# The modulation's last 2,176 bytes a row loaded in parts of 126, 2, 124 and 4 rows instead of 128

## Chip, cores, metric

One core of one Trainium2 chip. The metric is device time in microseconds (us), lower is better. A run counts as slow when it is over 1.5% above the fastest of the same kernel; such runs are left out of every comparison here.

## The reference

A decode block with adaptive layer norm: modulation, cached grouped attention over 8,192 keys, a gated MLP with ReLU gate. Cut to what matters:

```python
B, Sq, D = 8, 1, 1024; Hq, Hkv, Sk, Dh = 32, 4, 8192, 128; F = 3584
mod = (silu(c) @ w_mod).reshape(B, 6, 1, D)          # w_mod: 1024 x 6144, bf16
sa, ca, ga, sb, cb, gb = (mod[:, i] for i in range(6))
h = layernorm(x) * (1 + ca) + sa
x = x + ga * attention(h, k_cache, v_cache, wq, wo)
h = layernorm(x) * (1 + cb) + sb
x = x + gb * ((relu(h @ W_gate) * (h @ W_up)) @ W_down)
```

Everything is read once: 185.6 MB of weights and caches for a few KB of results.

## The kernel before

One ring of on-chip memory, the arena, takes all large operands in turn. Each is loaded with one instruction over all 128 partitions from the sync engine's queue, as soon as the part of the arena that it overwrites has been read. The chip has 16 DMA engines, and each of these loads is spread over all 16.

```python
wm_src = w_mod.rearrange("(p k) n -> p (k n)", k=KC)       # 128 rows of 98,304 bytes
load(("wm", 0), wm_src[:, 0:D], D, 0)                      #  2,048 bytes a row
load(("wm0", 0), wm_src[:, D:24 * D], 23 * D, D)           # 47,104
load(("wm", 1), wm_src[:, 24 * D:48 * D], 24 * D, 24 * D)  # 49,152
# ... then wq in two halves, for each batch K in two halves and V, then wo, gate, up
wd_parts = [(0, 14), (14, 21), (21, 25), (25, 27), (27, 28)]
for i, (r0, r1) in enumerate(wd_parts):                    # W_down last, in shrinking parts
    load(("wd", i), d_src[:, r0 * D:r1 * D], (r1 - r0) * D, VPART + r0 * D)
```

W_down's last 7 of 28 rows per partition are summed in a bank of their own, so that after the last load (2,048 bytes a row) only 8 small matmuls, two VectorE operations and the store are left.

## Time and profile before

| | before |
|---|---|
| time, first three runs | 436.42 us median (436.19 to 436.79) |
| profiled span | 434.9 us |
| share of the 16 DMA engines' time that the main queue fills | 99.0% |
| last load landed | 432.13 us |

The profile's page gives busy shares in 40 slices and the DMA queues; the view of windows gives busy time by stretch; the chain of waits lists what ended last. Beyond these views the trace keeps every DMA packet (start, duration, size, queue) and every landing, which is the time when one engine has finished its share of one load. A stretch without a packet in between is called a hole. Consecutive packets of one engine follow each other with a constant overlap of 4 ns, so the packets can be sorted into 16 sequences, one per engine. A sequence has no engine number in the trace.

### The profile page before, as it was taken

The page shows a single profiled execution, that of the slowest core. Times are in us where ns is not written, and L with a number is a line of the kernel's source. Part 1 is how long each engine was busy: PE and PEld are TensorE (multiplying, and loading weights), DVE is VectorE, ACT ScalarE, POOL GpSimd, SP SyncE. Part 2 cuts the span into 40 slices and gives each one's busy share as a digit, 9 for nine tenths or more (in the row PEclk, how much of TensorE's full clock was granted, in tenths as well). Part 3 has the DMA queues.
Part 4 walks back from the last instruction along what each step waited for, and adds up shares of the span by engine and source line. Part 5 has one row for each costly group of instructions (what it writes and reads, how often), then busy time and mean ns, then how long its engine had stood idle before and what let it go on. Part 6 is the DMA issues. An engine that isn't in the chain of part 4 may idle for free. (4 is left out here: it accounts for less than half of the span.)

```text
span 434.9 us, 4853 instructions
## 1 busy us (share of the span) xinstructions
PE 260.7 (60%) x2175; PEld 137.3 (32%) x2015; DVE 249.8 (57%) x345; ACT 29.8 (7%) x55; POOL 9.2 (2%) x24
## 2 busy tenths in 40 slices
PE   0325339566838874783977478487838856364247
PEld 0100003163218224421822352172226316241015
DVE  0603059747972985597299649739963974430021
ACT  1100010100020002002000200200020020100000
POOL 3000000000000000000000000000000000000000
PEclk9966569969978996998699599979968986885678
DMA  9999999989999999999999999999999999999996
GB/s 374 452 431 434 433 434 437 471 375 440 440 413 428 455 440 407 434 455 413 431 464 422 416 434 464 410 425 443 458 398 431 443 464 410 448 429 429 427 418 255
DMA packets 5526, 185.74 MB, mean 427 GB/s; under 512 B 720, under 2 KB 784, under 8 KB 1168
## 3 DMA queue, kind: packets, MB, share of 16 engines
q1 hardware_dynamic: 5376, 185.61, 99.0%
q8 instruction: 5, 0.08, 0.1%
q10 hardware_dynamic: 144, 0.04, 0.0%
q14 instruction: 1, 0.01, 0.0%
HBM read 185.63 MB, written 0.02 MB: 427 GB/s over the span
## 5 line engine op out<-in xcount | busy, mean ns | idle before, releaser
L584 DVE STREAM_TRANSPOSE kt<-arena 128x1024 uint32<-128x1024 uint32 x128 | 148.2, 1211 | 62.1 <-DVEq L181 44.7
L594 PE MATMUL ps<-kt,qpad 128*128 128x512 bf16 x512 | 133.9, 384 | 42.8 <-DVE kt L584 36.7
L634 PE MATMUL ps<-arena,pT 128*64 128x256 bf16 x1024 | 74.8, 321 | 51.0 <-PEq L181 51.0
L634 PEld LDWEIGHTS ps<-arena,pT 128*64 128x64 bf16 x1024 | 72.0, 132 | 53.2 <-issue 52.3
L594 PEld LDWEIGHTS ps<-kt,qpad 128*128 128x128 bf16 x512 | 40.5, 98 | 132.3 <-DVE kt L584 99.7
L624 DVE TENSOR_SCALAR pT<-pd,mqf 128x1024 bf16<-128x1024 bf16 x64 | 28.2, 503 | 0.6
L616 ACT ACTIVATE prb<-ps,bias 128x1024 bf16<-128x1024 f32 x16 | 17.7, 1110 | 138.8 <-DVE mjt L611 138.8
L622 DVE STREAM_TRANSPOSE pd<-prb 128x1024 bf16<-128x1024 bf16 x16 | 19.8, 1238 | 10.9 <-ACT prb L616 10.9
L600 DVE TENSOR_REDUCE negm<-ps 128x1 f32<-128x512 f32 x32 | 21.2, 661 | 4.5 <-PE ps L594 4.5
L762 PE MATMUL ps<-arena,hT 128*32 128x448 bf16 x128 | 10.7, 518 | 16.9 <-DMA arena<-in_B_W_up_dram 10.6
L769 DVE TENSOR_TENSOR kt<-ps,kt 128x448 bf16<-128x448 f32 x2 | 1.2, 620 | 27.8 <-PE ps L762 27.8
L546 PE MATMUL ps<-arena,hT 128*32 128x512 bf16 x64 | 7.2, 630 | 12.2 <-DMA arena<-in_A_wq_dram 12.2
L522 PE MATMUL ps<-arena,hT 128*32 128x512 bf16 x96 | 9.0, 551 | 8.2 <-DMA arena<-in_w_mod_dram 8.2
L653 ACT ACTIVATE oacc<-ps 128x32 f32 (+1 forms) x9 | 1.8, 198 | 158.6 <-PE ps L648 158.6
L575 POOL TENSOR_TENSOR qpad<-qR,mq 128x128 bf16<-128x128 bf16 x8 | 4.9, 607 | 310.7 <-DVE pT L624 258.2
L529 DVE COPY mod<-ps 128x512 f32<-128x512 f32 x2 | 1.3, 671 | 16.5 <-PE ps L522 16.5
L762 PEld LDWEIGHTS ps<-arena,hT 128*32 128x32 bf16 x64 | 2.3, 134 | 25.1 <-DMA arena<-in_B_W_up_dram 11.7
L557 DVE CAST kt<-ps 128x512 bf16<-128x512 f32 x1 | 0.7, 692 | 15.9 <-PE ps L546 15.9
L783 PE MATMUL ps<-arena,hmT 128*32 128x256 bf16 x84 | 6.4, 329 | 3.9 <-DMA arena<-in_B_W_down_dram 3.9
L606 PE MATMUL ps<-identf,negm 128*128 128x128 f32 x16 | 3.9, 326 | 7.8 <-DVE negm L604 7.8
L722 PE MATMUL ps<-arena,kt 128*32 128x256 bf16 x128 | 4.9, 328 | 4.6 <-DMA arena<-in_A_wo_dram 4.6
L546 PEld LDWEIGHTS ps<-arena,hT 128*32 128x32 bf16 x32 | 1.2, 137 | 18.2 <-DMA arena<-in_A_wq_dram 14.8
(99 smaller groups left out, 88.9 us busy)
## 6 DMA issues: line engine op xcount, KB each, us to landing
arena<-in_A_k_cache_dram SPq DMA_DIRECT2D x16, 4096.0 KB, 27.2
arena<-in_A_wq_dram SPq DMA_DIRECT2D x2, 4096.0 KB, 34.2
arena<-in_B_W_gate_dram SPq DMA_DIRECT2D x1, 7168.0 KB, 24.2
arena<-in_B_W_up_dram SPq DMA_DIRECT2D x1, 7168.0 KB, 28.8
arena<-in_w_mod_dram SPq DMA_DIRECT2D x1, 6144.0 KB, 30.4
arena<-in_w_mod_dram SPq DMA_DIRECT2D x1, 5888.0 KB, 16.5
arena<-in_B_W_down_dram SPq DMA_DIRECT2D x1, 3584.0 KB, 19.0
arena<-in_B_W_down_dram SPq DMA_DIRECT2D x1, 1792.0 KB, 22.9
```

Of the source, the lines that this page charges most:

```text
L522: fns.append(lambda e, w=w, pr=pr, j=j, kk=kk: hold(e.matmul(ps[32 * j:32 * j + 32, pr, :], hT[:, kk, :], w[:, 2 * pr:2 * pr + 2, j, :], s ...
L546: fns.append(lambda e, w=w, r=kk - r0, z=z, g=g, kk=kk: hold(e.matmul(ps[32 * g:32 * g + 32, 4 + z, :], hT[:, kk, :], w[:, r, g, z, :], st ...
L575: P.op("pool", lambda e: e.tensor_tensor(out=qpad[:, :, 24:152].rearrange("p u (q c) -> p u q c", q=4)[:, :, :, 0:J], in0=qR[:].rearrange( ...
L584: P.op("dve", lambda e_: e_.transpose(ktb[:, to:to + PART].bitcast(dt.uint32), arena[:, lo:lo + PART].bitcast(dt.uint32)), reads=[slot_r(l ...
L594: fns.append(lambda e_, t=t, r=r: e_.matmul(ps[:, e // 4, :].rearrange("p (c k) -> p c k", k=32), qpad[:, t * 2 + r, 24 - 8 * i:152 - 8 * ...
L600: P.op("dve", lambda e: e.tensor_reduce(negm[:, h:h + 1], ps[:, h, :], AX.X, ALU.max, negate=True), reads=[bank(h)] + (free(("ka", b)) if ...
L616: P.op("act", lambda e: e.activation(prb[:, f, :], ps[:, 2 * f:2 * f + 2, :].rearrange("p h n -> p (h n)"), ACT.Exp, bias=bias[:, 0:1], sc ...
L622: P.op("dve", lambda e: e.transpose(pd[:, f], prb[:, f]), reads=[R("prb", f, f + 1)], writes=[R("pd", 1024 * f, 1024 * f + 1024)])
L624: P.op("dve", lambda e, g=g: e.tensor_scalar(out=pT[:, f, :, :, g, :], in0=pd[:, f].rearrange("p (c i x) -> p c i x", c=32, i=2), scalar1= ...
L634: fns.append(lambda e, n=n, h=h, c_=c_, i=i, t=t: e.matmul(ps[64 * t:64 * t + 64, 5, 0:2 * Dh].rearrange("p (i d) -> p i d", d=Dh), pT[:, ...
L762: fns.append(lambda e, w=w, kk=kk, h=h, j=j, b0=b0: hold(e.matmul(ps[32 * j:32 * j + 32, b0 + h, 0:H], hT[:, kk, :], w[:, kk, j, h, :], st ...
L783: fns.append(lambda e, w=w, r=k - r0, k=k, i2=i2, j=j: e.matmul(ps[32 * j:32 * j + 32, 4, 0:256], hmT[:, k, 1 - i2:33 - i2], w[:, r, i2, j ...
```

## The change

The apparent intent: DMA engines 14 and 15 are to have less to move. Each load over 128 rows has one landing from each of the 16 engines and 8 packets on each; the last 2,176 bytes of each row are now loaded with row counts that do not divide evenly over 16 engines.

```diff
+    UNEVEN = [(832, 126), (256, 124)]          # bf16 elements a row, rows of the first part
 ...
-        load(("wm", 1), wm_src[:, 24 * D:48 * D], 24 * D, 24 * D)
+        at1 = 48 * D - sum(n for n, rows in UNEVEN)
+        load(("wm", 1), wm_src[:, 24 * D:at1], at1 - 24 * D, 24 * D)
+        for n, rows in UNEVEN:
+            for lo, part in ((0, slice(0, rows)), (n // 2, slice(rows, 128))):
+                load(("wm1", n, lo), wm_src[part, at1:at1 + n], n // 2, at1 + lo, arena[part, at1:at1 + n])
+            at1 += n
```

The rest of the diff hands a destination through the load helper. The two parts of a strip claim half of the strip's columns each in the kernel's own bookkeeping; the matmuls read all of them, so they wait for all four.

More of the change, by code (lines that the diff above doesn't have):

```diff
@@ L382, in bass_adaLN_cond__gqa_block_cached__glu_gated_reglu__decode_kernel, with load @@
         stream, place = [], {}
-        def load(key, src, n, lo):
+        def load(key, src, n, lo, dst=None):
             place[key] = lo
-            stream.append((key, src, n, lo))
+            stream.append((key, src, n, lo, arena[:, lo:lo + n] if dst is None else dst))
         def pump():
             while stream:
-                key, src, n, lo = stream[0]
+                key, src, n, lo, dst = stream[0]
                 if P.unread("arena", lo, lo + n):
@@ L393, in pump @@
                 stream.pop(0)
-                dst = arena[:, lo:lo + n]
                 P.op("sp", lambda e, dst=dst, src=src: e.dma_start(dst, src), writes=[slot_r(lo, lo + n)], dma=True,
```

## The prediction

> **What bounds the kernel now.** I read the page's header and its slices first. The DMA row shows nines from the second slice to the last but one and the compute engines stay far below that, so the 16 DMA engines are the candidate for the bound.
>
> ```profile
> span 434.9 us, 4853 instructions
> PE 260.7 (60%) x2175; PEld 137.3 (32%) x2015; DVE 249.8 (57%) x345; ACT 29.8 (7%) x55; POOL 9.2 (2%) x24
> DMA  9999999989999999999999999999999999999996
> ...
> q1 hardware_dynamic: 5376, 185.61, 99.0%
> q8 instruction: 5, 0.08, 0.1%
> q14 instruction: 1, 0.01, 0.0%
> ```
>
> To be seen here: one queue carries 185.61 MB in packets that fill 99.0% of all 16 engines' time, and beside it there are six small packets called instruction (five of 16,384 bytes, one of 8,192). The busy times by stretch agree: between 95 and 340 us the DMA share is 1.00 at 434 GB/s, PE is busy 170 us of 245 and VectorE 173.
>
> ```profile
> 95.00:340.00 245.00, 169.78 (x1293) 95.14 (x1288) 173.39 (x224) 15.19 (x31) 3.77 (x6) 0.89 1.00 434
> ```
>
> Then the DMA issue queue's own waits and its timeline, to see whether that queue ever runs dry. The gate weights are issued at 374.19 us and the transfer ahead of them (wo) lands at 381.27, so 7 us of work still stood in the rings; that lead is among the smallest. In the prologue the first half of K is issued at 36.40 us and wq's second half lands at 52.16; K's second half is issued at 55.84, when the first of the engines needs still 4.3 us for the half before it (its first share lands at 60.11). So compute never starves the DMA engines, and a shift of under 1 us in compute is absorbed.
>
> Last the chain that ended last and its timeline at the end.
>
> ```profile
> 405.43 24.84 DMA arena<-in_B_W_down_dram
> 430.26 0.04 issue
> 430.31 1.07 PE ps L792 x32
> 431.38 0.34 PE ps L746 x4
> 431.72 0.87 PE ps L792 x24
> 432.59 0.02 issue
> 432.61 0.29 DVE lu L803
> ```
>
> The pieces after the DMA are one short tail: W_down's last three loads land at 430.26, 431.49 and 432.13 us by the records of landings, PE ends at 432.6, two VectorE operations and the store finish at 434.83. The tail starts when the LAST of 16 engines has delivered its share. So the time is: the slowest DMA engine's stream plus a fixed tail of 2.7 us. What matters is therefore which engine is slowest, and that I read from the trace itself: every load has 16 landings (one per engine), and the packets of one engine follow each other so exactly (4 ns overlap) that the 16 sequences of 296 packets can be told apart.
>
> In the final load, 11 engines land by 430.94 or so and five much later: 431.97, 432.00, 432.10, 432.10, 432.13. All five delays have the same origin. At 46.40, 96.15, 386.53, 397.29 and 428.70 us one sequence, each time another, has a packet prolonged by 482 to 550 ns and then a hole of 861 to 935 ns, 1.42 us together; each is at one of the five 16,384-byte instruction packets (45.47, 95.28, 385.67, 396.35, 427.78). The 8,192-byte one (76.92) costs a sixth engine 0.83 us. The lost time is never made up, because the rings are never empty. The trace has no engine numbers, so I cannot see which numbers the five have.
>
> **What the Trainium skill says.** "Runtime: NRT & Kernel Launch", section Instruction fetch mechanics: instruction memories are refilled in 16 KiB blocks through a DMA queue driven by the sequencer. The trace agrees: five packets of exactly 16,384 bytes, on queues of their own. "DMA: Bandwidth & Descriptors", Queues, rings and completion order: each engine takes turns between its queues and the queues share the 16 engines. The trace agrees: one engine alone loses 1.42 us per fetch. Same page, Why a DMA increments its semaphore by 16 and not by 1: a load runs on the largest number of engines up to 16 that divides its row count, on the lowest-numbered ones; 128 rows use 16, 100 use 10, 127 use 1. All big loads here have 128 rows, so nothing in this trace shows the uneven case; the change rests on it.
>
> **The change part by part.** The third load (49,152 bytes a row) becomes 46,976 bytes a row, and the last 2,176 bytes a row come in two strips: 1,664 bytes in loads of 126 and 2 rows, 512 bytes in loads of 124 and 4. By the page's rule 126 rows go to 14 engines (0 to 13) with 9 rows each, 2 rows to engines 0 and 1, 124 rows to 4 engines (0 to 3) with 31 each, 4 rows to engines 0 to 3. The bytes in total do not change; only their place does.
>
> Cost of a packet, from this trace: 2,048 bytes take 84 ns, 4,096 take 159, 32,768 take 1,213, 65,536 take 2,418, with 4 ns overlap. That is about 5 ns plus bytes at 27.2 per ns net. So my estimates are 66 ns for 1,664 bytes, 24 for 512 (the 512-byte packets of the loads of c and x took 27), and 79 saved on each row of the shortened load. Per engine:
> - each saves 8 x 79 = 632 ns;
> - engines 0 and 1 get 10 x 66 + 32 x 24 = 1,428 ns, net +0.80 us;
> - engines 2 and 3 get 9 x 66 + 32 x 24 = 1,362 ns, net +0.73 us;
> - engines 4 to 13 get 9 x 66 = 594 ns, net -0.04 us;
> - engines 14 and 15 get nothing, net -0.63 us.
>
> The other additions: four more DMA issues, each 0.33 to 0.43 us of the issue queue as its other issues are, about 1.5 us, while the next one has to be there only when the ring runs out near 31 us; and four more semaphores for the second half of the modulation's matmuls. That half may start about 0.8 us later than its 31.54 us, since the loads land on four late engines; its end issues K's first half at 37.2 instead of 36.4, against rings that are full until past 50. No compute instruction is moved or removed; the order of all engines but the issue queue is the same. On the path that sets the end only the five late engines count:
> - if 14 or 15 is one of them, it leaves the late group, but three or four others still land at 432.0 to 432.1. The gain is at most 0.03 us even if both leave (432.13 less 432.10, the third-last landing), plus 0.04 for the packets;
> - if none of 0 to 3 is among them, those become late by 0.8 us, less than 1.42, and hide behind the late group.
> Sum in this case: -0.04 to -0.07 us, i.e. 436.4.
>
> **The rivals.**
> First: one of engines 0 to 3 carries an instruction fetch. Then its 0.73 to 0.80 us adds to the 1.42 and the end moves by the whole of it: 436.42 + 0.75 = 437.2. If five numbers out of 16 were drawn blindly, at least one of four would be hit in 82% of cases. Against that speaks the change's shape: it loads exactly those four with nearly what a fetch costs, which looks like a choice made by someone who had seen engine numbers. I give this 35%.
> Second: engine 14 stands out by more than the profiled execution shows, for example because two fetches fall on it in unprofiled runs. Then up to 0.6 us would be won, 435.8. Against it: the five delays here fall on five different sequences, and the profiled run (436.21) is as fast as the others (436.19 to 436.79), so its pattern is typical. 8%.
> Third: the shorter packets or odd row counts cost more than reckoned (holes at the ends of loads on few engines, unaligned rows). Even 32 packets at twice 27 ns add 0.8 us on engines 0 to 3 and would just pass the late group, by 0.2 us. A load of 126 rows falling on one engine alone would add about 126 x 66 ns = 8 us to that engine, near 443; the rule above speaks against it, 1%.
> Fourth: the transfer is hidden anyway and the change is lost in the spread of the runs (0.6 us between the three before). That is my main case with another name: the relief is real, but not on the engine that ends last.
>
> **Range and chances.** 56% for 436.3 to 436.5, 35% for about 437.2, 8% for 435.8 to 436.2. The median of this mix lies a little over 436.4; with the right tail heavier I say 436.5, with 436.0 to 437.4 to hold it 8 times in 10 (run to run spread of 0.3 us included). 2% are 8.7 us; nothing in the sum comes near. Faster by over 2%: 0.3%; within: 98.6%; slower: 1.1% (the one-engine case).
>
> **What would show it right or wrong.** In the changed trace the loads of 126 rows should show packets of 1,664 bytes on 14 sequences, nine or ten on each, and those of 124 rows 512-byte packets on four, 32 on each. Two sequences should run 0.63 us ahead of the middle from 31 us on and four 0.7 to 0.8 us behind, until the end. The five instruction packets should be there at the same times, each costing one sequence 1.42 us. The final load's last landing decides: near 432.1 with four or five engines in the late group, my main case; one to three engines landing near 432.8, the first rival; the last landing at 431.5, the second. I am wrong if the number of rows per sequence differs, if the fetches move to other engines, or if the issue queue falls behind at 31 us, shown as a hole in all sequences.

## The result

The changed kernel took 436.75 us in the median (436.38 to 437.46, 6 runs), the kernel before 436.43 (six runs, one of them slow at 444.64). The ratio of the fast runs is 1.0009, with a 95% interval of 0.9996 to 1.0023: the same at 2%, and slower by about 0.4 us if anything. (A ratio here is the mean time of one kernel's fast runs over that of the other's of the same rounds, so not quite the ratio of the medians.) In a later session on one chip it was 1.0025 (1.0005 to 1.0046): slower there, by far less than 2%. The time lies within the predicted range; the case that the prediction held likeliest, 436.3 to 436.5, is not what happened.

The page of the changed kernel, header, DMA row and queues, and its window of 95 to 340 us (the same lines of the kernel before stand in the prediction):

```profile
span 435.4 us, 4859 instructions
...
DMA  9999999999999999999999999999999999999995
...
q1 hardware_dynamic: 5656, 185.61, 98.9%
q8 instruction: 5, 0.08, 0.1%
...
q14 instruction: 1, 0.01, 0.0%
```

```profile
95.00:340.00 245.00, 168.94 (x1311) 94.59 (x1308) 173.37 (x224) 15.18 (x31) 3.77 (x6) 0.90 1.00 434
```

To be seen: the same bytes in 280 more packets, the same six instruction packets, and in the long middle the same 434 GB/s. What changed lies before 50 us and at the end. The chain of waits at the end (start, length, what):

```profile
424.67 6.33 PE ps L788 x84
430.99 0.93 PE ps L797 x32
431.93 0.03 issue
431.95 0.41 PE ps L751 x4
432.36 0.80 PE ps L797 x24
433.16 0.02 issue
433.18 0.29 DVE lu L808
```

Here PE runs without a wait from 424.67 us, because up's last share landed at 415.61 us instead of 415.11, and it still ends only 0.57 us later than before (433.16 for 432.59). The last landing moved about as much: 432.67 for 432.13, and PE's last eight matmuls start at 432.69, right behind it (before: 432.17). Up's last landing and this one come from the same latest engine.

The number of landings recorded for the four loads is 15, 3, 5 and 5, of which one each comes at 2.0 to 3.2 us, half a microsecond after the issue, when no data can have come. So 14, 2, 4 and 4 engines took part. That is what the prediction took from the Trainium skill, "DMA: Bandwidth & Descriptors", section Why a DMA increments its semaphore by 16 and not by 1, down to the rest of the 16 being written at once. Ends of the 16 sequences of packets, in us:

```
                                            before                                after
no instruction packet, not among 0 to 3     10 sequences, 430.19 to 430.60        6, 430.30 to 430.53; and 429.89
with 512-byte packets (engines 0 to 3)      -                                     431.16 431.16 431.37 and 432.37
with a 16,384-byte instruction packet       431.64 431.64 431.71 431.77 431.85    431.67 431.76 431.86 431.86 431.97
with the 8,192-byte one                     430.88                                (the 432.37 above)
```

The last engine in the changed kernel is one of 0 to 3, and it is the one that also carries the sixth, smaller instruction packet. Two other sequences received next to none of the 1,664-byte packets: one ends first of all (429.89), the other carries the instruction packet of 47 us and ends at 431.67.

### The profile page after: what moved, and what is told of

Its sections match the earlier page's. It is cut to its first block, busy times and chain, and to the rows that moved or that the text cites. A ratio compares the mean times of both kernels' runs of the same rounds, so it can differ in the third digit from the quotient of the medians.

```text
span 435.4 us, 4859 instructions
## 1 busy us (share of the span) xinstructions
PE 263.8 (61%) x2175; PEld 138.3 (32%) x2015; DVE 250.1 (57%) x345; ACT 29.8 (7%) x55; POOL 9.1 (2%) x24
## 5 line engine op out<-in xcount | busy, mean ns | idle before, releaser
L639 PE MATMUL ps<-arena,pT 128*64 128x256 bf16 x1024 | 72.7, 315 | 52.2 <-PEq L181 52.2
L639 PEld LDWEIGHTS ps<-arena,pT 128*64 128x64 bf16 x1024 | 70.3, 130 | 54.0 <-issue 53.5
L767 PE MATMUL ps<-arena,hT 128*32 128x448 bf16 x128 | 11.6, 555 | 14.9 <-DMA arena<-in_B_W_up_dram 11.1
L527 PE MATMUL ps<-arena,hT 128*32 128x512 bf16 x96 | 10.6, 631 | 8.6 <-DMA arena<-in_w_mod_dram 8.6
L551 PE MATMUL ps<-arena,hT 128*32 128x512 bf16 x64 | 6.9, 611 | 10.5 <-DMA arena<-in_A_wq_dram 10.5
L767 PEld LDWEIGHTS ps<-arena,hT 128*32 128x32 bf16 x64 | 2.4, 144 | 23.7 <-DMA arena<-in_B_W_up_dram 11.9
L727 PE MATMUL ps<-arena,kt 128*32 128x256 bf16 x128 | 6.1, 382 | 5.1 <-DMA arena<-in_A_wo_dram 5.1
L653 PEld LDWEIGHTS ps<-jmp,om 128*128 128x128 f32 x36 | 5.8, 205 | 4.1 <-DVE om L648 2.7
```

Of the source, the lines that this page charges most:

```text
L527: fns.append(lambda e, w=w, pr=pr, j=j, kk=kk: hold(e.matmul(ps[32 * j:32 * j + 32, pr, :], hT[:, kk, :], w[:, 2 * pr:2 * pr + 2, j, :], s ...
L551: fns.append(lambda e, w=w, r=kk - r0, z=z, g=g, kk=kk: hold(e.matmul(ps[32 * g:32 * g + 32, 4 + z, :], hT[:, kk, :], w[:, r, g, z, :], st ...
L639: fns.append(lambda e, n=n, h=h, c_=c_, i=i, t=t: e.matmul(ps[64 * t:64 * t + 64, 5, 0:2 * Dh].rearrange("p (i d) -> p i d", d=Dh), pT[:, ...
L727: fns.append(lambda e, w=w, k=k, j=j: e.matmul(ps[32 * j:32 * j + 32, 5, 0:256], oX[:, k, :], w[:, k, j, :], start=(k == 0), stop=(k == KO ...
L767: fns.append(lambda e, w=w, kk=kk, h=h, j=j, b0=b0: hold(e.matmul(ps[32 * j:32 * j + 32, b0 + h, 0:H], hT[:, kk, :], w[:, kk, j, h, :], st ...
```

## The experiments

Twelve runs, all correct, beside the kernel before. Three theories, in the words of the expectations: A, engine 3's instruction packet adds to its extra load; B, the odd loads cost every engine time; C, spread. S, U and R came later: is B due to small packets just ahead of wq (S), to unequal shares (U), or to cutting a load over its rows (R)?

To judge B, each packet's duration is compared with 8.5 ns plus its bytes at 27.2 per ns, which fits the undisturbed packets of 512 bytes and more within 1 ns. The excess over 15 ns, summed over the packets that start in a stretch and divided by 16, is the time that a mean engine loses; packets prolonged by an instruction packet are to be left out, but of 71 and 38 in the last column some 35 are such. All traces, in ns:

```
                                     8-20 us   29.5-33.5   33.5-46   50-95   profiled run, us
before                                   18          0         0      357     436.21
c1 before again                           1          0         0        6     436.12
d1 strips of 128 rows                     0          0         0        0     436.28
r3 only 124 + 4                           0         30         0       37     436.62
after                                     4        487         0        0     436.75
r2 only 126 + 2                           0        327         0        0     436.84
c3 126 + 2, 122 + 6                      12        714        41        0     436.52
d3 126 + 2, after the second load       288          0         0        0     436.14
d2 all four, after the second load      424          0         0        0     437.21
e1 112 + 16                            1102        460         0        0     437.88
c2 126 + 2, aligned                       0        764      1766        0     439.72
c4 126 + 2, double 124 + 4                0        907      1309       38     438.80
r1 after again                         1077        677      1353       71     439.44
r4 marked before                          0        324        96       70     438.57
```

### The changed kernel again

No edit.

> The changed kernel once more, with more rounds and a second trace. Theory A (an engine among 0 to 3, which the small rows load by 0.8 to 1.1 us, also carries the 8,192-byte instruction packet of about 0.88 us, so that it ends 2.0 us behind the middle and passes the engines with a 16,384-byte packet at 1.42 us): slower than before by 0.3 to 0.6 us, about 436.9, and in the trace the last sequence of packets is again one with 32 packets of 512 bytes. Theory B (the odd loads cost time for everyone, by slow packets near 31 us and the later start of the modulation's second half): also slower, but the last sequence may be any, and the middle of the landings is late as well by 0.3 us or more at the end. Theory C (nothing but the spread of runs): ratio 1.000 within 0.0005.

Measured: 436.29, 436.45, 438.22, 438.72 and 439.44 us (and one slow run of 483.54), the kernel before 435.99 to 436.98 in 11 runs, ratio 1.0025 (1.0005 to 1.0046). That is more than any theory said. The trace is of the slowest of these and shows all engines slow for long stretches. Views of windows (stretch, length, busy time of PE, weight loads, VectorE, ScalarE, GpSimd, clock, DMA share, GB/s), first before, then this run:

```profile
33.00:47.00 14.00, 6.96 (x72) 0.90 (x24) 3.39 (x7) 0.60 (x1) 0.00 (x0) 0.62 1.04 448
52.00:95.00 43.00, 25.78 (x152) 10.89 (x138) 30.11 (x40) 4.38 (x7) 1.08 (x2) 0.79 1.00 427
```

```profile
33.00:47.00 14.00, 7.40 (x72) 1.14 (x32) 3.39 (x7) 0.60 (x1) 0.00 (x0) 0.62 1.00 383
52.00:95.00 43.00, 22.35 (x108) 7.61 (x94) 29.31 (x39) 4.38 (x7) 1.08 (x2) 0.78 1.01 435
```

The DMA share is 1.04 before and 1.00 here, the rate 383 for 448 GB/s: the engines are never without work, each packet takes longer. After 52 us the rate is as before. The landings of the last load have six engines within 0.32 us (435.06 to 435.38), so engine 3 did not stand out here: its sequence was 0.5 us behind the middle when attention began, not 1.1, and 1.4 after its instruction packet. A holds for the first trace and not for this one; B has more to it than A.

### Each strip alone

```diff
-    UNEVEN = [(832, 126), (256, 124)]
+    UNEVEN = [(832, 126)]            # r2_only_126
+    UNEVEN = [(256, 124)]            # r3_only_124
```

> Only the strip of 1,664 bytes a row in loads of 126 and 2 rows; the 512-byte strip goes back to the big load. Theory A: engines 0 to 3 are then loaded by under 0.15 us more than the rest, the late group of 16,384-byte packets sets the end again: within 0.1 us of before, 436.4. Theory B: 126 rows on 14 engines and slow packets near 31 us remain, so most of the 0.4 us loss remains, 436.7 to 436.8. Theory C: 436.4.

Measured: 436.21 to 437.88 us in the five fast runs, ratio 1.0017 (1.0001 to 1.0033). The trace has 327 ns of slowness right behind the strip. Engines 0 to 3 were hardly loaded and yet it is slower: against A alone, for B.

> Only the strip of 512 bytes a row in loads of 124 and 4 rows: engines 0 to 3 get 32 packets of some 24 ns for 8 x 19 ns saved, so about +0.62 us; the others -0.15 us. Theory A: the engine with the 8,192-byte packet ends at 0.88 + 0.62 = 1.5 us plus its own early delay, against 1.27 for the late group: slower than before by 0.1 to 0.3 us, 436.5 to 436.7, and 512-byte packets on the last sequence. Theory B: some of the loss, 0.2 us, with any sequence last. Theory C: 436.4.

Measured: 435.94, 436.00, 436.14, 436.62 and 438.90 us, ratio 1.001 (0.9987 to 1.0033), unresolved. Only 30 ns of slowness. Four sequences are 0.7 us behind the others, as reckoned (0.77 by the estimate of +0.62 and -0.15), but the last engine is neither of these: it carries the instruction packet of 46 us and came 0.6 us late out of the first three loads, and ends at 432.01. A's expectation of a 512-byte packet on the last sequence failed.

### Which engine carries which packet

The kernel before with 15 tiny loads behind its third load, of 1 to 15 rows, so that the sizes on a sequence name its engine.

```diff
+        for r in range(1, 16):       # 144 to 368 bytes a row, into a tile that nothing reads
+            P.op("sp", lambda e, ...: e.dma_start(mark[0:r, at1:at1 + n], w_mod[0:r, 0:n]), ..., dma=True)
```

> The kernel before with 15 tiny loads after its third load, of 1 to 15 rows, one row per engine on the lowest-numbered engines, each load of its own row size (144 to 368 bytes), so that the sizes on a sequence of packets name its engine. It costs engine 0 about 0.25 us and engine 15 nothing. Theory A: the 8,192-byte instruction packet lies on one of engines 0 to 3, the five of 16,384 bytes on five engines from 4 to 15, one of them 14 or 15; time within 0.2 us of before. If a 16,384-byte packet lies on 0 to 3, theory A is wrong in that the engine is fixed. Theories B and C say nothing of it.

Measured: all 120 tiny packets sort into 15 chains of sizes that each begin at another row count and run to the end (5, 6, ... 15 on engine 4), plus one sequence with none (engine 15). So the lowest-numbered engines took the rows in this trace. The instruction packets and the sequences that lose time beside them:

```
packet at, us   bytes    engine
48.65           16,384   14
79.50            8,192    3
97.42           16,384    5
387.94          16,384    6
400.88          16,384    8
430.44          16,384   not resolved (the tail's short packets cannot be sorted); not 0 to 3 in the trace of "after"
```

A's engines are right. The tiny loads cost more than reckoned (two runs, 438.57 and 440.62 us): holes of 0.2 to 0.4 us between tiny loads on three engines, and slow packets for all others. The marked kernel is good for its numbers, not for its time.

Engine 14 is also one of the two that the change relieves. In the trace of before its sequence is the one with the packet at 46.40 us and ends last, at 431.85, 0.08 us behind the next; in the control below 0.34 us behind the next, with even strips 0.28, with the 124-row strip alone 0.66.

### Control: the kernel before, submitted as a change

> The kernel before, unchanged, submitted as if it were a change. If the wide times of the first batch (up to 439 us, and 483 to 486 once each) come from the way a submitted kernel is run or from the chip, this one shows them too: some of its 6 runs over 437. If they come from the odd loads, its runs lie within 435.9 to 437.0 as those of the kernel before did. Ratio 1.000 in both cases for the undisturbed runs. In its trace engine 14's fetch (near 46 to 48 us) and four others of 1.42 us form the late group.

Measured: 435.77 to 436.28 us in 5 runs, ratio 0.9997 (0.9983 to 1.001). The long times of the first batch do not come from the way a kernel is run. Its trace has no slow spell at all, which makes it the better reference than the first one, which lost 357 ns between 50 and 95 us.

### The strip aligned

```diff
+    UNEVEN = [(1024, 126)]
```

> The 126-row strip alone, but of 2,048 bytes a row beginning at a multiple of 256 bytes, where the strip of 1,664 and the shortened big load begin and end at odd multiples of 128. If the general slow spell at 30 to 32 us (0.33 us per engine with the 1,664-byte strip alone, 0.45 with both strips, 0.03 with the 512-byte strip, none before) comes from the alignment, it is below 0.1 us here and the undisturbed runs are at 436.0 to 436.1, as before. If it comes from 126 rows on 14 engines, it is 0.3 or more and the undisturbed runs stay at 436.2 to 436.4.

Measured: 436.32 to 436.84 us and 439.72, ratio 1.0008 (0.9994 to 1.0021); 764 ns of slowness at 30 us and 1.77 us more up to 46 us in the profiled run. The alignment isn't it. Some 0.8 us of this run is another thing, the tail, of which more below.

### Engine 3 spared

```diff
+    UNEVEN = [(832, 126), (128, 122)]
```

> The 1,664-byte strip as in the change; the second strip is 256 bytes a row in loads of 122 and 6 rows, so that engines 0 and 1 get 61 rows each (61 x 13 to 16 ns, about 0.8 to 1.0 us) and engines 2 and 3 next to none. Theory A (engine 3 with the 8,192-byte packet and the load ends last): here engine 3 ends 0.9 us behind the middle and not 2.0, engines 0 and 1 about 1.0; the late group of 1.42 to 1.52 sets the end and 0.3 to 0.5 us are won back against the changed kernel: undisturbed runs at 436.0 to 436.2. Theory B (slow spells for all): 436.3 as the changed kernel's.

Measured: engine 3's sequence ends at 431.71, not last, and the last four (431.98 to 432.08) carry 16,384-byte packets, which is A's part. But nothing was won: 436.35 to 437.91 us, ratio 1.002 (1.0008 to 1.0033), with 714 ns of slowness. The end of the chain of waits shows it waiting for the DMA again:

```profile
404.33 26.30 DMA arena<-in_B_W_down_dram
430.63 0.04 issue
430.67 1.07 PE ps L797 x32
```

A is true of which engine comes last and too small to explain the time.

### The second strip doubled

```diff
+    UNEVEN = [(832, 126), (512, 124)]
```

> The second strip doubled, 1,024 bytes a row in loads of 124 and 4 rows: engines 0 to 3 get 32 packets of some 43 ns, 8 x 38 ns less in the big load, about +1.1 us with the first strip's share, others -0.3. Theory A: engine 3 ends 0.88 + 1.1 + 0.3 = 2.3 us behind the middle or more; the end moves by 0.3 to 0.5 us against the changed kernel, undisturbed runs near 436.7. Theory B: as the changed kernel, 436.3.

Measured: 437.19, 438.70 and 438.80 us fast (three more slow), ratio 1.0039 (1.0021 to 1.0058), more than A's 436.7. Engine 3 stood 2.1 us behind the middle at 190 us, but in the profiled run 2.2 us of slowness of all engines outweigh that. Inconclusive for the dose of A.

### Strips with all 128 rows

```diff
+    UNEVEN = [(832, 128), (256, 128)]      # one load each, same place, same bytes
```

> The same two strips of 1,664 and 512 bytes at the same place, but each in one load of all 128 rows, so every engine gets 8 rows of each and none is relieved. Where do the slow spells after 30 us come from (all 16 engines at once, 0.3 to 3 us in the traces of the changed kernel, of the 1,664-byte strip and of the tiny loads, never in the kernel before)? Theory U (unevenness: the engines enter wq's load apart by 0.6 to 1.5 us): no spell here, excess at 30 to 32 us under 0.1 us, all runs within 435.9 to 437.0. Theory S (small packets just ahead of wq): spells as in the changed kernel, some runs over 437. Packet cost by itself: 8 x (66 + 24) less 8 x 79, under 0.1 us. Theory A expects 436.2.

Measured: 436.01 to 436.75 us and one of 437.63, ratio 0.9995 (0.9957 to 1.0033; the interval is wide, as a run of before at 441.09 us counts as fast), and no slowness in the trace. Its window, to be held against the one of the repeated change:

```profile
33.00:47.00 14.00, 7.12 (x72) 0.96 (x24) 3.39 (x7) 0.60 (x1) 0.00 (x0) 0.62 1.04 446
```

446 GB/s, as before (448). Two more small loads ahead of wq cost nothing that can be seen. S is out, by this one trace.

### The loads moved ahead

```diff
-  (strips at the end of the third load)
+  at1 = 24 * D - sum(n for n, rows in UNEVEN)    # strips at the end of the second load,
+  load(("wm0", 0), wm_src[:, D:at1], at1 - D, D)  # the third load whole
```

> The change's four loads moved to the end of the second load (the modulation's first half), so that 49,152-byte rows of the modulation follow them and not wq. If the spells belong to wq entered unevenly: the engines still enter wq apart (the lead and lag of engines lasts), so spells at 30 us and later remain and times reach 437 to 439. If they belong to odd loads followed by anything: a spell at 16 us. If they belong to small packets directly ahead of wq: none, times 436.3 to 436.7, with engine 3 last at about 2.0 us behind the middle by theory A.

Measured: 436.39 to 437.21 us and 442.43 (and one slow run of 480.78), ratio 1.0029, interval 0.9967 to 1.009, unresolved. The trace's slowness moved along: 405 ns at 15 to 20 us, none at 30. So it follows the cut loads and is not a property of wq. A further 0.8 us of this profiled run lies in PE's tail.

> Only the 1,664-byte strip in loads of 126 and 2 rows, at the end of the second load. It relieves engine 14, which ended last in the traces of the kernel before (by 0.08 us in one, 0.34 in the other), without loading engine 3. If no spell comes: 0.05 to 0.3 us faster than before, 435.9 to 436.1, the last landing on another engine with a 16,384-byte packet. If spells come: 436.3 to 438, slower.

Measured: 436.14 to 436.99 us, ratio 0.9991 (0.9954 to 1.0028), unresolved; 288 ns of slowness at 15 to 20 us; the last five landings within 0.11 us (431.98 to 432.09). With engine 14 relieved and engine 3 hardly loaded, the other engines with instruction packets set the end, as the prediction had it, and no gain can be shown.

### Cut over the rows, but evenly

```diff
+    UNEVEN = [(832, 112)]            # 112 + 16 rows: 7 + 1 on every engine
```

> The 1,664-byte strip in loads of 112 and 16 rows: both row counts are multiples of 16, so every engine gets 7 rows and 1, 8 in all, as in an even load, and none is relieved or loaded; but the load is cut into two over the rows, as in the change. The strips of 126 and 2 rows showed a slow spell of all engines of 0.27 to 0.33 us right behind them in three traces, at 16 or at 30 us, and the even strips of 128 rows none. If it is the unequal number of rows per engine (theory U), none here: excess at 30 to 32 us under 0.1 us, undisturbed runs at 436.0 to 436.2, spread as before. If it is the cut over the rows, which gives a row to another engine than the one that moves it in a load of 128 rows (theory R), a spell of 0.2 us or more is here too and the runs lie at 436.3 and more.

Measured: 436.32 to 436.80 us and 437.88 in the profiled run, ratio 1.0008 (0.9992 to 1.0024). Every engine took part in both loads and had 8 rows in all, and the spell is there: 460 ns at 31 to 33 us. So the slow spell does not need unequal shares (U), and R stands, on this one trace. The spell comes behind loads cut over the rows, with 112 + 16 as with 126 + 2, and not behind loads of the same strips over 128 rows. Two things speak against a rule as plain as that: 124 + 4 rows of 512 bytes are cut as well and lost 30 ns, and the 15 tiny loads of the marked kernel, of 1 to 15 rows each, lost 324. And one thing mars this trace, a second spell of 1.1 us at 8 to 20 us, before its cut loads moved any data; the repeated change shows the same one. Its five other runs, 0.3 us or so over before's (435.87 to 436.72), are the second sign, within the interval.

## Why the prediction was right or wrong

**The range was right, and so was "within 2%".** That is part luck: the sum had -0.04 to -0.07 us and the measured change is +0.3, and the range was wide enough to hold a failed step and a missing term that it was not reckoned from. By the prediction's own signs the trace is nearest to the first rival: one engine lands last, at 432.67 (the sign was 432.8). The bound (the slowest DMA engine's stream, then 2.7 us of tail) held in both kernels' traces: between last landing and end lie 2.7 us before (434.83 less 432.13) and 2.74 after (435.41 less 432.67). It did not hold in all: by the spans, the tail is 2.73 to 2.76 us in ten traces of 14, 3.0 in r3 and r4, and 3.5 in c2 and d2. In d2 the last landing is at 432.37, but PE, at a granted clock of 0.65 between 424 and 432 us (before: 0.79), starts its last eight matmuls only at 433.21. With slow spells and tail together the profiled times of d2 and c2 are accounted for within 0.2 us of the control's 436.12 (0.42 + 0.8 of 1.1 us; 2.7 + 0.8 of 3.6).

**Which engines take which rows: right.** 14, 2, 4 and 4 engines by the landings, the lowest-numbered by the marked kernel.

**The packet costs: right.** 1,664 bytes took 69 ns (reckoned 70 gross), 46,976 bytes 1,735 for the 1,815 of 49,152 (80 saved, reckoned 79). The 512-byte packets took 27 in the traces without a spell on them (r3, d1), and 32 in the median in the changed kernel, inside its spell. In the first trace, engines 0 to 3 stood 0.77, 0.78, 0.97 and 1.10 us behind the middle at 62 us; reckoned as a distance to the middle were 0.77 and 0.84.

**The relief: right, and worth nothing that could be measured.** Of the two relieved sequences one ends first. Engine 14 was indeed the last engine, and with it off the end, three or four others stand within 0.1 to 0.3 us.

**The step that failed: "those become late by 0.8 us, less than 1.42, and hide behind the late group".** The text had itself counted a sixth engine with a loss of 0.83 us and then dropped it from the case. It also misread its line: of the final load's landings before, ten are in by 430.87 us and the eleventh comes at 431.19, not all eleven "by 430.94 or so". That eleventh is the engine of the 8,192-byte packet, engine 3. With 1.10 us of load and 0.88 us of its packet it stood 2.0 us behind the middle and ended 0.40 us after the next engine. The first rival was in the same spirit but named the wrong packet: no engine from 0 to 3 carries one of 16,384 bytes.

**The term that was missing: the slow spell.** No part of the sum held that all 16 engines would run slow behind the cut loads. The third rival came closest (cost of odd row counts), but placed it on engines 0 to 3. It measured 0.29 to 0.9 us in every trace with a strip of 126 or 112 rows, and none with 128.

**A size that was off, without effect.** The modulation's second half was to start 0.8 us later; it started at 33.29 us for 31.54, and K's first half was issued at 38.64 for 36.40 (reckoned 37.2). The load ahead of K landed only at 52.43 us, so nothing came of it.

**The sum, from the two traces without other disturbance** (the control and the change): the middle of the sequences without instruction packet ends at 429.98 us in the one and 430.36 in the other, +0.38; the last sequence lies 1.78 us behind the middle in the one (engine 14) and 2.02 in the other (engine 3), +0.24. Together +0.62, and the last landings differ by 0.63 (432.04 and 432.67). So the larger part is the shift of the middle, which the 0.49 us of slow spell in the table covers. Against the first trace of before (+0.54) it was hidden, since that trace happened to lose 0.36 us later on.

**What stays open.** Why a load cut over rows is followed by a slow spell isn't settled. The Trainium skill, "DMA: Bandwidth & Descriptors", section The descriptor swizzle, says that in a load over 128 partitions each engine writes through one port of the on-chip memory; a cut that gives rows to other engines would end that. It may fit, but no run shows which port was written, nor whether reading or writing is slow, and it would not tell why 124 + 4 rows lost next to nothing. Nor is it known why some executions go on being slow up to 47 to 50 us (after 46 us another 0.17, 0.29 and 0.38 us in c2, c4 and r1, which the table leaves out). Runs over 437 us, fast: 3 of 41 of the kernel before, 17 of 53 of the kernels with cut loads, 1 of 6 with even strips. So long times are commoner with cut loads, yet two of the long spells began at 8 us, ahead of any cut data.

## What to carry to other kernels

When the DMA engines are the bound, the end waits for the slowest of 16, so list all 16 with everything that each carries, small instruction packets too, before loading some to relieve another. A relief of one engine is worth only the distance to the next late one, here 0.08 to 0.34 us. A row count that moves the shares can change more than the shares: test the cut with equal shares, as with 112 and 16 rows, before reckoning with bytes alone. And before a difference of under 1 us is put down to a load, see whether the compute tail behind the last landing was as long in both runs.

## What the Trainium skill lacked or had wrong

- "Runtime: NRT & Kernel Launch", Instruction fetch mechanics, calls the cost of crossing a 16 KiB boundary "mostly hidden", and does not say what it costs the DMA engine that carries the block. In this kernel, which is bound by DMA, each such packet costs that engine 1.42 us of its stream (a packet prolonged by 482 to 550 ns and a hole of 861 to 935), and five of 16 engines end 1.2 to 1.5 us behind the others.
- "DMA: Bandwidth & Descriptors", Latency and other measured facts, says that engines 7 and 15 are usually slower, with a best guess that concerns loads issued from GpSimd. The loads here are issued from the sync engine, so this is no contradiction: the late ones were 14, 5, 6, 8, one not resolved and, in the changed kernel, 3, each by its instruction packet; engine 15 carried none.
- No page has the spell behind loads cut over rows: 0.29 to 0.9 us lost by a mean engine behind parts of 126 + 2 or 112 + 16 rows, 0.32 behind loads of 1 to 15 rows, 0.00 behind two loads of 128 rows with the same bytes, and 0.03 behind 124 + 4 rows of 512 bytes.
- The rule for the number of engines (same page, Why a DMA increments its semaphore by 16 and not by 1) was confirmed for 126, 124, 4 and 2 rows, so nothing is wrong there: 14, 4, 4 and 2 engines by their landings.
